# Quad 5's k and q: loaded earlier and transposed by DMA instead of TensorE

## The chip, the cores and the metric

The kernel runs on one core of a Trainium2 chip. The metric is the device time of one execution in microseconds. Of the kernel before there are three timed runs, and one more execution that the profiler recorded; the profile's own times count from the start of its span.

## The reference

Sigmoid attention over 8 batches, 12 heads, 448 positions and 64 dimensions per head, and behind it two matrix products with a SiLU between them. All inputs and the output are float32.

```python
def _attn_ref(q, k, v):
    S = q.shape[2]
    scale = 1.0 / np.sqrt(q.shape[-1])
    scores = scale * np.matmul(q, k.transpose(0, 1, 3, 2)) - np.log(S)
    attn = 1.0 / (1.0 + np.exp(-scores))
    return np.matmul(attn, v)

x = attn_out.transpose(0, 2, 1, 3).reshape(B * S, H * D)    # 3584 x 768
h = x @ w_in                                                # 768 x 2048
g = h * (1.0 / (1.0 + np.exp(-h)))
out = g @ w_out                                             # 2048 x 768
```

## The kernel before

**Quads.** Four heads of one batch are a *quad*; a batch has three (`NQ`), the whole problem 24. A quad's k, q and v are loaded (`load`, line 124, on GpSimd's DMA queue, with a cast to 16 bits) into tiles `kf`, `qf` and `vf`, three of each in rotation (`p3`): quad 5's tiles are those that quad 2 had, and quad 8's are those that quad 5 had.

**Transposes.** The scores need k and q with the head dimension on the partitions (`kT`, `qT`, three of each in rotation). There are two ways to get there. `pe_transpose` (line 196) multiplies the 14 blocks of a tile with the identity on TensorE into two PSUM banks, and two VectorE casts (line 203) move them to `kT` or `qT`. `dma_transpose` copies the tile once into another order of its elements (`kr`, `qr`, line 211, two of each in rotation), and a DMA on SP's queue (line 212) transposes that copy into `kT` or `qT`. Quads 0 to 5 take the first way, quads 6 to 23 the second.

**Units.** A quad has seven *units*, one per 64 keys. `scores` (line 225) makes one: four matmuls into a double PSUM bank `psc`, of which there are two in rotation in the first stage, and one ScalarE sigmoid (line 232) into `attnT`. `values` (line 256) multiplies the seven units of a quad with v, 28 matmuls into two single PSUM banks `pav`, and VectorE scales the sums into `xT` (line 267). Four single banks are in rotation in this stage, for `ptrk`, `ptrq`, `pav` and `ph`.

**h.** `h_unit` (line 288) makes one block of 128 of the 2048 columns of h for one batch: six matmuls of a part of w_in with `xT` into a bank `ph`. The last two of the six need the batch's third quad. For batch 0 ScalarE makes a sigmoid of the bank (`tx`, line 302) and VectorE multiplies the two (`gTr`, line 303), which frees the bank; for batch 1 ScalarE does it alone (SiLU, line 307). w_in is loaded in four quarters (`load_w_in`, line 155, four transfers each); the second quarter, `load_w_in(1)`, serves blocks 4 to 7.

**Order.** Every engine runs its instructions in the order in which the program emits them. In the first stage that order is a table: units 0 to 23 one by one (`for n in range(NT_B + 3)`), each followed by what `behind` lists for its number; there lie the transposes of quads 1 to 4, the values of quads 0 to 2 in pieces, and the first matmuls of h blocks 0 and 1 (`begin`). From unit 24 to unit 41 come *bursts* of two units (`burst`), each followed by the values of a finished quad, if there is one, and by eight or nine h matmuls (`stretch`). Quad 5's first unit is unit 35, the second of burst n=34. The transposes of quad 5 stood behind bursts n=26 (k) and n=30 (q). Loads are called from `after_transpose(g)` and `after_values(g)`, so their place on GpSimd's queue follows the places of those steps in the program; a load also waits until the tile it overwrites has been read.

After unit 41 and the values of quad 5, the rest of batch 0's and batch 1's h blocks follow; in between stand VectorE's sums of parts of w_in and w_out (`w_in_sums`, line 326, and `w_sums`, line 477) and the row copies of quads 6 to 8. Then come three stages in which the output products (`out_set`, line 504) of one pair of batches alternate with the scores and values of the next, each followed by the next pair's h (`h_pair`, line 378), and at the end the output products of the last pair.

Of the kernel before, what the change touches and what calls it, by code (L numbers as in the profile page):

```python
# [17 lines left out]
def kernel(  # L18
# [9 lines left out]
    nc = tc.nc  # L28
# [82 lines left out]
    def new_flat(name, g):  # L111
        flat[name, g] = p3.tile([P, 2, NCH, D], F16, tag=f"{name}f", name=f"{name}f")

    def rows_in(name, g):
        b, iq = divmod(g, NQ)
        return source[name][b, 4 * iq : 4 * iq + 4].rearrange(
            "(i h) (p c) d -> (h p) i (c d)", h=2, c=NCH
        )

    def load(names, g, c0=0, c1=NCH):  # L120
        for name in names:
            if (name, g) not in flat:
                new_flat(name, g)
            nc.gpsimd.dma_start(  # L124
                flat[name, g][:, :, c0:c1].rearrange("p i c d -> p i (c d)"),
                rows_in(name, g)[:, :, c0 * D : c1 * D],
            )
# [22 lines left out]
    def load_w_in(step):  # L150
        cols = slice(step * DFF // 4, (step + 1) * DFF // 4)
        rows = moe_w_in[:, cols].rearrange("(iq j h d) f -> h j d iq f", j=2, h=2, d=D)
        for half in range(2):
            for j in range(2):
                nc.gpsimd.dma_start(
                    w_in_sb[j * D : (j + 1) * D, half * NQ : (half + 1) * NQ, cols], rows[half, j]
                )
# [13 lines left out]
    def new_qkT(g):  # L171
        for name in ("k", "q"):
            qkT[name, g] = p3.tile([P, NCH, P], F16, tag=f"{name}T", name=f"{name}T")
# [14 lines left out]
    def pe_transpose(g, pieces=(("k", 0, 4), ("k", 4, NCH), ("q", 0, 4), ("q", 4, NCH))):  # L188
        if ("k", g) not in qkT:
            new_qkT(g)  # L190
        for name, c0, c1, *copy in pieces:
            dst = qkT[name, g].rearrange("p c t -> p (c t)")
            ptr = one_bank(f"ptr{name}")
            for c in range(c0, c1):
                for j in range(2):
                    nc.tensor.matmul(
                        ptr[j * D : (j + 1) * D, (c - c0) * P : (c - c0 + 1) * P],
                        flat[name, g][:, j, c, :],
                        ident,
                        start=True,  # L200
                        stop=True,
                    )
            (copy[0] if copy else nc.vector.tensor_copy)(  # L203
                dst[:, c0 * P : c1 * P], ptr[:, : (c1 - c0) * P]
            )

    def dma_transpose(g, name, copy):
        if ("k", g) not in qkT:
            new_qkT(g)
        rows = p2.tile([P, NCH, 2, D], F16, tag=f"{name}r", name=f"{name}r")  # L210
        copy(rows, flat[name, g].rearrange("p j c d -> p c j d"))
        nc.sync.dma_start_transpose(
            out=qkT[name, g], in_=rows.rearrange("p c j d -> p (c j d)")
        )
# [25 lines left out]
    def values(g, end=NCH):  # L240
        b, iq = divmod(g, NQ)
        if b not in xT:
            assert b < 2 or b - 2 in h_done
            xT[b] = p2.tile([P, NPAIR, S], F16, tag="xT", name="xT")
        pav, done_rounds = part_of.pop(g, None) or (None, 0)
        if pav is None and bufs_of["double"] > 2 and "any" not in banks:
            both = two_banks("pav")
            pav = [both[:, half] for half in range(2)]
        elif pav is None:
            pav = [one_bank("pav") for _ in range(2)]  # L250
        for ch in range(done_rounds, end):
            at = attnT.pop((g, ch))
            for half in range(2):
                own = slice(half * HP, (half + 1) * HP)
                for j in range(2):
                    nc.tensor.matmul(  # L256
                        pav[half][j * D : (j + 1) * D, :S],
                        flat["v", g][own, j, ch, :],
                        at[own, j, :],
                        start=(ch == 0),  # L260
                        stop=(ch == NCH - 1),
                    )
        if end < NCH:
            part_of[g] = pav, end
            return
        for half in range(2):
            nc.vector.tensor_scalar_mul(xT[b][:, half * NQ + iq, :], pav[half][:, :S], SX)  # L267
        if iq == NQ - 1:
            ready.add(b)
# [365 lines left out]
    def after_transpose(g):  # L635
        if g == 0:
            load("kq", 3)
        elif g == 1:
            load("kq", 4)
            load_w_in(0)  # L640
            load_w_in(1)
        elif g == 2:
            load("kq", 5)
        elif g == 5:
            load("kq", 8)

    def after_values(g):
        if g == 0:
            load("v", 3)
            load_w_in(2)  # L650
            load_w_in(3)
        elif g == 1:
            load("v", 4)
            load_w_out(0, 0)
            load_w_out(0, 1)
        elif g == 2:
            load("v", 5)
            load_w_out(1, 0)
            load_w_out(1, 1)
            load("kq", 6)  # L660
            load("kq", 7)
        elif g + 3 < NQB:
            load("v", g + 3)
        if g >= 2 * NQ and g % (2 * NQ) == 2 * NQ - 2:
            sums_of_x.append(x_sums(g // (2 * NQ), 0, NQ - 1))
# [14 lines left out]
    def rest_of_first_k():  # L680
        pe_transpose(0, (("k", FIRST, 4), ("k", 4, NCH)))
        after_transpose(0)

    def transposes(g, name):
        pe_transpose(g, ((name, 0, 4), (name, 4, NCH)))
        if name == "q":
            after_transpose(g)

    def rounds(g, end):
        values(g, end)  # L690
        if end == NCH:
            after_values(g)

    def begin(fc, steps):
# [11 lines left out]
        8: ((transposes, 2, "k"),),  # L706
        9: ((transposes, 2, "q"),),
        10: ((rounds, 0, 3),),
        11: ((rounds, 0, 7),),
        12: ((transposes, 3, "k"),),  # L710
        13: ((transposes, 3, "q"),),
        14: ((rounds, 1, 2),),
        15: ((rounds, 1, 4),),
        16: ((rounds, 1, 7),),
# [1 line left out]
        18: ((transposes, 4, "q"),),  # L716
        19: ((rounds, 2, 3),),
        20: ((rounds, 2, 6),),
        21: ((begin, 0, 4),),
        22: ((rounds, 2, 7),),  # L720
        23: ((begin, 1, 4),),
    }
    for n in range(NT_B + 3):
# [6 lines left out]
    def stretch(stream, ns, spent=0):  # L730
        nonlocal done, due
        due += ns
        done += spent
        while done < due:
            step_ns = next(stream, None)
            if step_ns is None:
                return
            done += step_ns

    def burst(n, size=2):  # L740

        new = units[n : n + size]
        for u in new:
            scores(*u)
        with_values = values_if_any()
        for g, ch in new:
            if ch == NCH - 1:
                waiting.append(g)
                if 9 <= g + 3 < NQB:
                    later.extend(((g + 3, "k"), (g + 3, "q")))  # L750
        return with_values
# [2 lines left out]
    stretch(stream, 1600)  # L754
    for n in range(NT_B + 3, 2 * NT_B, 2):
        burst(n)
        if n in (26, 30):
            transposes(5, "k" if n == 26 else "q")
        stretch(stream, 1600)
    values_if_any()  # L760
    for _ in stream:
# [5 lines left out]
    for m in range(B // 2 - 1):  # L767
# [11 lines left out]
        left, n = 0.0, 2 * NT_B * (m + 1)  # L779
# [62 lines left out]
```

## Time and profile before

| what | value |
|---|---|
| three timed runs | 368.84, 369.35, 369.56 us, median 369.35 |
| profiled execution: its own time | 369.54 us |
| its span in the profile | 367.6 us |
| granted TensorE clock | full over the whole span |
| data moved by DMA | 42.78 MB, mean 116 GB/s |
| scores' sigmoid (line 232) | 168 instructions, 1009 ns each |
| h matmul (line 288) | 192 instructions, 353 ns each, overlapping |
| k and q DMA transposes (line 212) | 18 each, median 3.5 us (k) and 4.6 us (q) to landing |

The first stage, with everything up to the last h block of batch 1, ends near 76 us. Busy times per engine over parts of it, in us, with what the DMA engines moved:

| stretch, us | TensorE | VectorE | ScalarE | DMA, GB/s |
|---|---|---|---|---|
| 20 to 25 | 4.93 | 3.97 | 5.00 | 203 |
| 25 to 30 | 5.00 | 1.69 | 4.89 | 204 |
| 30 to 35 | 4.63 | 2.73 | 4.35 | 202 |
| 35 to 40 | 5.00 | 2.79 | 3.79 | 203 |
| 40 to 45 | 5.00 | 2.31 | 4.65 | 207 |
| 45 to 50 | 4.56 | 2.85 | 4.54 | 202 |
| 50 to 55 | 5.00 | 2.75 | 4.03 | 204 |

A timeline line gives the start, the length from the first start to the last end, the engine, the source line and the operation with what it writes and reads. Lengths of neighbours on one engine overlap, so what a piece of work takes from its engine is read from start to start. What an engine waited for stands in brackets behind the line. "To landing" is the time from the issue of a transfer to its end.

### The profile page before, as it was taken

To read this page: it belongs to the slowest core of one execution; us is meant where nothing else is said; L and a number is where in the kernel's file an instruction comes from. 1 tells how busy PE (TensorE), PEld (TensorE's weight loads), DVE (VectorE), ACT (ScalarE), POOL (GpSimd) and SP (SyncE) were. 2 spreads that over 40 slices of the span, in tenths; PEclk is the share of its full clock that TensorE was granted. 3 is DMA by queue.
4 is the path that set the end of the run, shared out by engine and by line. 5 is a ranking of instruction groups with operands and counts; after the bars stand their busy time and mean duration, and the time that the engine had idled before them with its cause. 6 is when DMAs were issued, how large, how long until landed. Compare 5 with 4: busy or idle time off the path is not lost. (4 is left out here: it accounts for less than half of the span.)

```text
span 367.6 us, 7594 instructions
## 1 busy us (share of the span) xinstructions
PE 359.3 (98%) x3009; PEld 183.8 (50%) x3009; DVE 251.8 (69%) x458; ACT 250.0 (68%) x339; POOL 77.5 (21%) x116
## 2 busy tenths in 40 slices
PE   7999999999999999999999999999999999999995
PEld 3554445545544555545445555554455555555552
DVE  2565559957756587867665768795756677797763
ACT  5998886479998756687777846679998956640000
POOL 8566521040061172000041047000100000000000
PEclk9999999999999999999999999999999999999999
DMA  8999999987989599007589359922863020003333
GB/s 132 198 204 202 204 203 204 197 115 134 153 114 223 117 135 177 2 0 162 92 168 206 61 128 129 135 24 51 151 113 86 19 71 0 3 0 86 87 86 85
DMA packets 65858, 42.78 MB, mean 116 GB/s; under 512 B 36128, under 2 KB 62496, under 8 KB 65824
## 3 DMA queue, kind: packets, MB, share of 16 engines
q0 software_dynamic: 27072, 22.58, 43.0%
q1 hardware_dynamic: 38320, 19.34, 27.0%
q8 instruction: 23, 0.38, 0.4%
q10 hardware_dynamic: 432, 0.39, 0.3%
q14 instruction: 11, 0.09, 0.1%
HBM read 45.61 MB, written 11.01 MB: 154 GB/s over the span
## 5 line engine op out<-in xcount | busy, mean ns | idle before, releaser
L232 ACT ACTIVATE attnT<-psc,bias_s 128x896 f16<-128x896 f32 x168 | 158.1, 1009 | 21.9 <-PE psc L225 21.6
L504 PEld LDWEIGHTS <-S 128*128 128x128 f16 x448 | 41.3, 98 | 36.5 <-issue 8.1
L225 PE MATMUL psc<-qT,kT 64*64 64x448 f16 x672 | 51.1, 362 | 1.4 <-DVE kT L203 0.5
L267 DVE TENSOR_SCALAR xT<-pav 128x448 f16<-128x448 f32 x48 | 27.7, 619 | 32.5 <-PE pav L256 32.5
L124 POOL DMA_DIRECT2D vf<-in_v_dram x24 | 17.3, 721 | 136.0 <-PE pav L256 118.1
L504 PEld LDWEIGHTS <-gTr 128*128 128x128 f16 x336 | 31.3, 98 | 26.6 <-issue 7.7
L504 PE MATMUL po<-T,S 128*128 128x384 f16 x224 | 42.0, 327 | 0.2
L504 PE MATMUL po<-w_out_sb,gTr 128*128 128x384 f16 x224 | 41.6, 327 | 0.0
L378 PEld LDWEIGHTS <-w_in_sb 128*128 128x128 f16 x288 | 27.9, 98 | 26.7 <-issue 1.1
L504 PE MATMUL po<-w_out_sb,S 128*128 128x384 f16 x224 | 40.8, 326 | 0.0
L256 PE MATMUL pav<-attnT,vf 64*64 64x448 f16 x672 | 38.3, 350 | 0.5 <-DVE gTr L303 0.4
L288 PE MATMUL ph<-xT,w_in_sb 128*128 128x448 f16 x192 | 38.7, 353 | 0.1
L378 PE MATMUL pa<-xT,w_in_sb 128*128 128x448 f16 x144 | 33.1, 353 | 0.0
L225 PEld LDWEIGHTS <-kT 64*64 64x64 f16 x672 | 17.8, 104 | 28.7 <-issue 22.3
L378 PEld LDWEIGHTS <-SI 128*128 128x128 f16 x216 | 21.1, 98 | 20.0 <-issue 0.5
L256 PEld LDWEIGHTS <-vf 64*64 64x64 f16 x672 | 21.0, 107 | 13.3 <-issue 3.8
L288 PEld LDWEIGHTS <-w_in_sb 128*128 128x128 f16 x192 | 17.8, 98 | 19.1 <-issue 3.7
L394 ACT ACTIVATE part<-pa 128x448 f32<-128x448 f32 x24 | 13.1, 544 | 19.2 <-PE pa L378 18.3
L504 PE MATMUL po<-T,gTr 128*128 128x384 f16 x112 | 22.1, 327 | 0.0
L372 ACT ACTIVATE gTr<-pc 128x448 f16<-128x448 f32 x24 | 13.1, 544 | 12.9 <-DVE pc L388 12.5
L388 DVE TENSOR_TENSOR part<-pb,part 128x448 f32<-128x448 f32 x24 | 14.9, 621 | 8.3 <-ACT part L394 5.0
L186 ACT ACTIVATE m<-po 128x384 f32<-128x384 f32 x1 | 0.5, 491 | 27.7 <-PE po L504 27.7
(75 smaller groups left out, 468.2 us busy)
## 6 DMA issues: line engine op xcount, KB each, us to landing
out_dram<-osb SPq DMA_DIRECT2D x52, 192.0 KB, 3.0
vf<-in_v_dram POOLq DMA_DIRECT2D x24, 224.0 KB, 6.5
kf<-in_k_dram POOLq DMA_DIRECT2D x23, 224.0 KB, 6.9
qf<-in_q_dram POOLq DMA_DIRECT2D x23, 224.0 KB, 7.4
w_in_sb<-in_moe_w_in_dram POOLq DMA_DIRECT2D x16, 192.0 KB, 8.1
w_out_sb<-in_moe_w_out_dram POOLq DMA_DIRECT2D x4, 768.0 KB, 14.9
out_dram<-osb SPq DMA_DIRECT2D x6, 96.0 KB, 2.1
kT<-kr SPq DMA_TRANSPOSE x18, 3.5
```

The lines of the kernel that those rows point to most:

```text
L124: nc.gpsimd.dma_start(flat[name, g][:, :, c0:c1].rearrange("p i c d -> p i (c d)"), rows_in(name, g)[:, :, c0 * D : c1 * D],)
L186: nc.scalar.activation(o, i, AF.Copy)
L225: nc.tensor.matmul(psc[own, j, :S], qkT["k", g][rows, ch, own], qkT["q", g][rows, :, own], start=True, stop=True,)
L232: nc.scalar.activation(attnT[g, ch], psc[:, :, :S], AF.Sigmoid, bias=bias_s, scale=QKSCALE)
L256: nc.tensor.matmul(pav[half][j * D : (j + 1) * D, :S], flat["v", g][own, j, ch, :], at[own, j, :], start=(ch == 0), stop=(ch == NCH - 1),)
L267: nc.vector.tensor_scalar_mul(xT[b][:, half * NQ + iq, :], pav[half][:, :S], SX)
L288: nc.tensor.matmul(ph[:, :S], w_in_sb[:, cc, fc * P : (fc + 1) * P], xT[b][:, cc, :], start=(at == 0), stop=(at == NCC - 1),)
L372: nc.scalar.activation(gTr[:, r * NG + i, col + c * S : col + (c + 1) * S], h, AF.Silu, bias=0.0, scale=ISX)
L378: nc.tensor.matmul(to, w[:, n, i * P : (i + 1) * P], x[:, n], start=(start and n == 0), skip_group_check=not start, stop=(n == NQ - 1),)
L388: nc.vector.tensor_add(o, po, x)
L394: nc.scalar.activation(got[i, 1], bank[i, "a"], AF.Copy)
L504: nc.tensor.matmul(po[:, :NO2], a[:, fc, :], w[:, fc, :], start=(fc == 0), stop=(fc == NHC - 1))
```

## The change

The second quarter of w_in is issued behind quad 5's k and q instead of ahead of them. Quad 5 no longer passes through TensorE: VectorE copies its k rows ahead of the scaling of quad 2 and its q rows behind it (`rows_of_5`, in the places of units 21 and 22), and SP's queue transposes both. Behind the q rows stands `after_transpose(5)`, which loads quad 8's k and q; that call moves with it from burst n=30 to unit 22, so on GpSimd's queue these two loads now stand ahead of the load of quad 6's v.

```diff
@@ after_transpose
         elif g == 1:
             load("kq", 4)
             load_w_in(0)
-            load_w_in(1)
         elif g == 2:
             load("kq", 5)
+            load_w_in(1)
         elif g == 5:
             load("kq", 8)
@@
+    def rows_of_5(name):
+        dma_transpose(5, name, nc.vector.tensor_copy)
+        if name == "q":
+            after_transpose(5)
@@ behind
         18: ((transposes, 4, "q"),),
         19: ((rounds, 2, 3),),
         20: ((rounds, 2, 6),),
-        21: ((begin, 0, 4),),
-        22: ((rounds, 2, 7),),
+        21: ((rows_of_5, "k"), (begin, 0, 4)),
+        22: ((rounds, 2, 7), (rows_of_5, "q")),
         23: ((begin, 1, 4),),
@@
     for n in range(NT_B + 3, 2 * NT_B, 2):
         burst(n)
-        if n in (26, 30):
-            transposes(5, "k" if n == 26 else "q")
         stretch(stream, 1600)
```

## The prediction

> **What bounds the kernel now.** I read the busy shares first, then TensorE's waits, then each engine's timeline over the stretch that the edit touches (20 to 60 us), then the transfers.
>
> ```profile
> span 367.6 us, 7594 instructions
> ...
> PE 359.3 (98%) x3009; PEld 183.8 (50%) x3009; DVE 251.8 (69%) x458; ACT 250.0 (68%) x339; POOL 77.5 (21%) x116
> ```
>
> TensorE has work for 98% of the span, so what is taken out of its order shows up at the end, unless another engine then holds it. Its list of waits has six entries for the whole span, and two of them lie in the stretch:
>
> ```profile
> PE pav L256 <- DVE gTr L303: 0.4, 1, 0.4
> PE ptrk L196 <- DVE gTr L303: 0.4, 1, 0.4
> ```
>
> The second waits inside the transposes that go away. TensorE's timeline (start, length, work):
>
> ```profile
> 32.51 0.71 PE L225 MATMUL psc<-qT,kT 64*64 64x448 f16 x8
> 33.16 0.41 PE L196 MATMUL ptrk<-ident,kf 128*64 128x128 f16 x8
> 33.94 0.36 PE L196 MATMUL ptrk<-ident,kf 128*64 128x128 f16 x6 [0.37 <-DVE gTr L303]
> 34.23 1.88 PE L288 MATMUL ph<-xT,w_in_sb 128*128 128x448 f16 x9
> ...
> 39.98 0.58 PE L196 MATMUL ptrq<-ident,qf 128*64 128x128 f16 x14
> 40.50 1.88 PE L288 MATMUL ph<-xT,w_in_sb 128*128 128x448 f16 x9
> ...
> 44.43 0.66 PE L225 MATMUL psc<-qT,kT 64*64 64x448 f16 x8
> ...
> 48.02 1.51 PE L256 MATMUL pav<-attnT,vf 64*64 64x448 f16 x26 [0.44 <-DVE gTr L303]
> ```
>
> The k transposes hold TensorE from 33.16 to 34.23 (1.07 us, wait included), the q transposes from 39.98 to 40.50 (0.52 us). The burst at 44.43 (n=34) is the first with a unit of quad 5. ScalarE in the same stretch:
>
> ```profile
> 35.38 0.55 ACT L302 ACTIVATE tx<-ph 128x448 f16<-128x448 f32 x1
> 36.47 1.91 ACT L232 ACTIVATE attnT<-psc,bias_s 128x896 f16<-128x896 f32 x2 [0.54 <-PE psc L225]
> ...
> 42.74 1.91 ACT L232 ACTIVATE attnT<-psc,bias_s 128x896 f16<-128x896 f32 x2 [0.35 <-PE psc L225]
> ...
> 46.74 1.01 ACT L302 ACTIVATE tx<-ph 128x448 f16<-128x448 f32 x2
> ```
>
> It is nearly as full as TensorE: its waits on the bursts are only 0.54 and 0.35 us. The wait of 0.44 us at TensorE's 48.02 is ScalarE's doing: that bank holds h block 9, which VectorE (L303) can release only after the sigmoid at 46.74.
>
> **The change, part by part.** *Removed:* 28 matmuls and 28 weight loads, four PSUM banks taken, and four VectorE casts (two pairs of 1.15 us). TensorE's order shortens by 1.07 + 0.52 = 1.59 us, the upper bound of the gain.
>
> How much ScalarE lets through I work out burst by burst. Two score banks take turns, so a burst's second unit waits for the second sigmoid of the burst before; a sigmoid is 0.95 us and the short one 0.45 us from start to start.
> - n=28, now at 36.03, comes up at 34.96. Its second unit waits for the sigmoid that ends at 35.46. The short sigmoid then runs to 35.9, so the pair of n=28 starts at 35.83 instead of 36.47. TensorE goes on to the values about 35.7 instead of 36.44: 0.74 of the 1.07 us is left.
> - n=30 comes at 38.7; behind it the h matmuls follow at 39.24 instead of 40.50. n=32 comes at 41.1, but ScalarE still has the pair of n=30 (39.3 to 41.2) and a short one to do: the pair of n=32 starts at 41.7 instead of 42.74, without its 0.35 us of idle time.
> - n=34 would come at 43.2; its second unit waits for 43.6. The pair of n=34 runs 44.05 to 45.95 instead of 44.96 to 46.88, the short sigmoid of block 9 starts at 45.95, VectorE releases the bank at 47.1, and TensorE goes on at 47.1 instead of 48.02.
>
> So from 48 us on **0.9 us** remain: ScalarE's two idle times, 0.54 + 0.35. Behind that each pair has at least 0.5 us of room (bursts 2.3 to 4.3 us apart), and from 57 us TensorE waits for nobody. The four missing banks shift the ring of four by two between n=26 and n=30 and then bring it round again, so block 9 meets the same bank. I take 0.9, ends 0.5 and 1.6.
>
> *Added on VectorE:* two copies, by their own row 0.61 us, in the holes around quad 2's scaling:
>
> ```profile
> 24.23 1.14 DVE L203 CAST qT<-ptrq 128x512 f16<-128x512 f32 x2
> 27.58 1.16 DVE L267 TENSOR_SCALAR xT<-pav 128x448 f16<-128x448 f32 x2 [2.20 <-PE pav L256]
> 29.84 1.15 DVE L303 SCALAR_TENSOR_TENSOR gTr<-ph,tx 128x448 f16<-128x448 f32 x2 [1.10 <-ACT tx L302]
> ...
> 62.44 0.61 DVE L211 COPY kr<-kf 128x896 f16<-128x896 f16 x1
> ```
>
> The k copy has 25.37 to 27.58, the q copy 28.74 to 29.84: hidden if quad 5's k lands by 26.9 and q by 29.2. Behind a late k copy the scaling waits, and h block 0's last two matmuls (at about 28.5) wait for that, one us for one.
>
> *Moved on POOL's queue:* quad 5's two loads go ahead of w_in(1)'s four. The queue keeps eight transfers in flight; each issue waits for the one eight before it.
>
> ```profile
> 17.50 0.63 POOL L155 DMA_DIRECT2D w_in_sb<-in_moe_w_in_dram  x1 [0.61 <-DMA kf<-in_k_dram]
> ...
> 22.22 0.74 POOL L124 DMA_DIRECT2D kf<-in_k_dram  x1 [0.24 <-PE pav L256]
> ```
>
> In the 17.50 and 18.57 places k and q land about where w_in(1)'s first two did (25.4, 26.4) plus 32 KB each: 25.6 and 26.8. Their buffers were quad 2's, transposed by 16.4. w_in(1)'s four then land at 27.7 to 30.7 instead of 25.4 to 28.5: 448 KB at the 203 GB/s of this stretch is 2.25 us. Block 4's first matmul, the last before burst n=26, wants the first half at 32.3; its second, behind that burst, wants the rest at 33.2.
>
> *Added on SP:* two transposes, at about 26.4 and 29.4, on a queue otherwise empty until 62 us. In 62 to 72 us, where they run beside loads, all traffic together keeps the loads' rate:
>
> ```profile
> DMA packets 5672, 2.05 MB, mean 205 GB/s; under 512 B 4659, under 2 KB 5672, under 8 KB 5672
> ```
>
> So each displaces 224 KB, 1.1 us: w_in(1) ends by 31.8, v of quad 3 lands at 32.1 + 2.3 = 34.4 (wanted at 35.7), w_in(2) at 38.3 (wanted at 40.4), v of quad 5 at 52.1 (wanted at 54.6). The first two transposes of that later stretch landed in 5.6 and 4.9 us, all of them in 2.9 to 13.7: k at 32, q at 35, wanted at 43.6.
> The Trainium skill, page "VectorE: DVE Perf Modes", section "The three transpose paths", puts a 128x128 transpose at 390 ns on TensorE and 1309 ns by DMA, and advises TensorE where PSUM will do. By its figure seven blocks are an estimated 9.2 us, both tiles 18.3 us, so q would land at 44.7 and burst n=34 wait 1.1 us, an end of 369.5 us; the landings of 5.6 and 4.9 us do not agree.
>
> *Moved too:* quad 8's two loads go ahead of v of quad 6 on POOL's queue. v of quad 6 is issued near 57.5 instead of 49.18 and, at the 8.6 us of its neighbours, lands at 66; its values start at 85.9. Quad 6's loads land near 61.5 by the displaced 2.3 us (59.1 now); VectorE may wait 0.7 us for them, but it has 3.84 us of idle time at 73.6.
>
> **Sum.** The profiled execution took 369.54 us, 1.94 more than its span: 369.54 - 0.9 = 368.64. The median of the runs, 369.35, lies 0.19 below it, so I predict 369.35 - 0.9 = **368.45 us**.
>
> **Rivals.** *All of it:* ScalarE does not hold TensorE, since h blocks or score banks pace differently from my starts: 369.35 - 1.59 = 367.75. For it: TensorE's 98%. Against: ScalarE's gaps add up to less.
> *Half is given back:* ScalarE, full from 35 to 47 us, catches up only with the values, so q's 0.52 is wholly lost and part of k's too: 369.35 - 0.5 = 368.85. For it: bursts n=30 to 36 come 2.1 to 2.8 us apart against ScalarE's 2.4 to 2.8 us of work.
> *Quad 5's q lands late:* the longest q landing, 12.0 us, gives 41.4, still ahead of 43.6; it decides from 14.2 us on. At 15.3 us it gives back 1.1: 369.55.
> *Slower, by loads pushed back:* if a transpose costs the loads three times its bytes while both run (3.4 us instead of 1.1), w_in(1) ends at 34.1 and TensorE waits 0.9 us at block 4; v of quad 3 lands at 39.0 against 36.6, 2.4 us more: 369.35 - 0.9 + 3.3 = 371.75. It decides from about 1.8 us each (v of quad 3 at 35.7); at 2.7 us TensorE waits 0.2 and 1.6 us, +0.9 in all, 370.25. Against: 205 GB/s beside transposes. For it: all margins here are 1.3 us.
> *Slower, because the load is no earlier:* if k lands at its old 29.4, the scaling starts at 30.0 instead of 27.58: 369.35 - 0.9 + 2.4 = 370.85. Against: landings in the stretch are 7.1 to 8.7 us, and 9.4 would be needed.
>
> **How the numbers follow.** Forecast 0.45, all of it 0.12, half 0.18, q late 0.05, loads pushed back 0.14, load no earlier 0.06. About 0.2% (0.74 us) is what a measurement can tell from no change, so faster is below 368.6. The forecast lies just below that line and run-to-run differences put a fifth of it above: faster 0.36 + 0.12 + 0.04 of "half" = 0.52; same 0.09 + 0.14 + 0.05 = 0.28; slower 0.20. The range runs from 367.6 (all of it, and 0.15 of scatter) to 370.4 (loads pushed back at 2.7 us, and the same scatter), which leaves out the worst of the two slow cases and little below. The forecast's own range is 368.0 to 368.9.
>
> **What would show it.** In the profile after: no L196 work past 24 us; k copies of quad 5 near 25.7 and the scaling still at 27.6; the pair of sigmoids of n=28 near 35.8; TensorE's wait before the values of quad 4 still there, ending near 47.1; first product (L504) near 75.1 instead of 75.97; span near 366.7. I am wrong if TensorE waits on w_in_sb or vf at 32 to 36 us, on kT or qT near 43.6, or if the scaling starts after 28 us.

## The result and the profile after

| | before | after |
|---|---|---|
| median of 22 runs each | 369.48 us | 370.07 us |
| ratio of the times, 95% interval | | 1.0020 (1.0011 to 1.0028) |
| profiled execution: own time, span | 369.54, 367.6 us | 371.07, 369.0 us |
| first h matmul behind the values of quad 5 | 57.01 us | 55.88 us |
| first output product | 75.97 us | 75.64 us |
| output product ahead of quad 6's values | 84.59 us | 86.11 us |

The change made the kernel slower by 0.2%. One of the 22 executions after, 411.1 us at a granted clock of 0.85, is left out of the ratio. The profiled execution lies 1.0 us above the median of its kernel, so the late waits in it are larger than in a typical one; it shows where they are. TensorE's work, from its timeline, before and then after:

```profile
57.01 19.13 PE L288 MATMUL ph<-xT,w_in_sb 128*128 128x448 f16 x99
75.97 2.44 PE L504 MATMUL po<-w_out_sb,gTr 128*128 128x384 f16 x14
...
79.18 1.30 PE L504 MATMUL po<-T,S 128*128 128x384 f16 x7
...
84.59 0.98 PE L504 MATMUL po<-w_out_sb,S 128*128 128x384 f16 x5
```

```profile
55.88 19.13 PE L288 MATMUL ph<-xT,w_in_sb 128*128 128x448 f16 x99
75.64 2.44 PE L504 MATMUL po<-w_out_sb,gTr 128*128 128x384 f16 x14 [0.63 <-ACT gTr L307]
...
79.25 1.31 PE L504 MATMUL po<-T,S 128*128 128x384 f16 x7 [0.25 <-DVE S L515]
...
86.11 0.97 PE L504 MATMUL po<-w_out_sb,S 128*128 128x384 f16 x5 [1.27 <-DVE osb L528]
```

TensorE was 1.13 us ahead of the kernel before at 56 us. Ahead of the first output product 0.80 of it went, at the third product (79.25, before 79.18) nothing of it was left, and the wait at 86.11 put it 1.52 us behind. That distance it kept, about: 1.4 us at the end of the span. So the stage that was changed got faster, and the three waits behind it gave more than that back. VectorE's timeline after shows what was late:

```profile
25.81 0.62 DVE L211 COPY kr<-kf 128x896 f16<-128x896 f16 x1 [0.37 <-DMA kf<-in_k_dram]
27.64 1.16 DVE L267 TENSOR_SCALAR xT<-pav 128x448 f16<-128x448 f32 x2 [1.21 <-PE pav L256]
...
61.40 0.56 DVE L477 TENSOR_TENSOR T<-w_out_sb 128x768 f16<-128x768 f16 x1 [1.42 <-DMA w_out_sb<-in_moe_w_out_dram]
...
63.30 0.62 DVE L211 COPY kr<-kf 128x896 f16<-128x896 f16 x1 [0.40 <-DMA kf<-in_k_dram]
...
73.33 0.62 DVE L211 COPY kr<-kf 128x896 f16<-128x896 f16 x1 [4.08 <-DMA kT<-kr]
...
84.98 0.62 DVE L211 COPY kr<-kf 128x896 f16<-128x896 f16 x1 [1.77 <-DMA kf<-in_k_dram]
```

Quad 5's k copy fits its hole, and the scaling starts at 27.64, on time. The third copy below (73.33) is quad 8's: it overwrites the rows of quad 6, two of each being in rotation, and so waits 4.08 us for quad 6's transpose. All of `w_sums` that stands behind it is late. Before, that wait was 0.47 us:

```profile
68.84 0.62 DVE L211 COPY kr<-kf 128x896 f16<-128x896 f16 x1 [0.47 <-DMA kT<-kr]
```

The gate on GpSimd's queue is a copy of one element of quad 8's `qT`; the loads of quads 9 to 11 stand behind it. SP's queue after, and the gate after and then before:

```profile
26.52 1.32 SPq L212 DMA_TRANSPOSE kT<-kr  x1
29.35 3.93 SPq L212 DMA_TRANSPOSE qT<-qr  x1
64.01 1.22 SPq L212 DMA_TRANSPOSE kT<-kr  x1
65.32 3.63 SPq L212 DMA_TRANSPOSE qT<-qr  x1
69.04 3.78 SPq L212 DMA_TRANSPOSE kT<-kr  x1
```
```profile
78.63 1.55 POOL L568 COPY gate<-qT 1x1 f16<-1x1 f16 x1 [14.10 <-DMA qT<-qr]
```
```profile
74.03 0.18 POOL L568 COPY gate<-qT 1x1 f16<-1x1 f16 x1 [13.67 <-DMA qT<-qr]
```

Quad 6's two transposes landed 9.2 and 8.7 us after issue; before it was 5.6 and 4.9. The k transpose, before and then after:

```profile
kT<-kr SPq DMA_TRANSPOSE x1, 5.6
```
```profile
kT<-kr SPq DMA_TRANSPOSE x1, 9.2
```

The gate, which waits for quad 8's, opened at 78.63 instead of 74.03, and quad 9's k was issued at 80.12 instead of 74.51. VectorE waited 1.77 us for that load at 84.98, with the sum of line 528 queued behind the copy, and TensorE waited 1.27 us for the bank that this sum reads. The added transposes themselves (times to landing, k and q of quad 5):

```profile
kT<-kr SPq DMA_TRANSPOSE x1, 11.5
...
qT<-qr SPq DMA_TRANSPOSE x1, 14.5
```

### The profile page after: what moved, and what is told of

Its sections match the earlier page's. It is cut to its first block, busy times and chain, and to the rows that moved or that the text cites. A ratio compares the mean times of both kernels' runs of the same rounds, so it can differ in the third digit from the quotient of the medians.

```text
span 369.0 us, 7541 instructions
## 1 busy us (share of the span) xinstructions
PE 359.0 (97%) x2981; PEld 183.1 (50%) x2981; DVE 250.9 (68%) x456; ACT 250.0 (68%) x339; POOL 78.8 (21%) x116
## 5 line engine op out<-in xcount | busy, mean ns | idle before, releaser
L124 POOL DMA_DIRECT2D kf<-in_k_dram x25 | 18.0, 722 | 8.9 <-DMA w_out_sb<-in_moe_w_out_dram 3.4
```

The lines of the kernel that those rows point to most:

```text
L124: nc.gpsimd.dma_start(flat[name, g][:, :, c0:c1].rearrange("p i c d -> p i (c d)"), rows_in(name, g)[:, :, c0 * D : c1 * D],)
```

## The experiments

Each was timed against the kernel before on the same chip (369.38 to 369.49 us there, so that a difference between runs of two chips carries up to 0.11 us from that).

| run | median, us | ratio to before, 95% interval |
|---|---|---|
| no transposes of quad 5 | 368.91 | 0.9991 (0.9982 to 1.0000) |
| no transposes, spare bank | 368.21 | 0.9969 (0.9958 to 0.9980) |
| changed, spare bank | 369.69 | 1.0008 (0.9996 to 1.0020) |
| changed, own rows for quad 8 | 369.44 | 1.0009 (0.9992 to 1.0026) |
| changed, v of quads 6 to 8 deferred | 369.11 | 0.9988 (0.9979 to 0.9997) |
| changed, v deferred, spare bank | 368.42 | 0.9968 (0.9957 to 0.9978) |
| before, two more transposes | 370.21 | 1.0020 (1.0011 to 1.0029) |
| before, load order alone | 369.45 | 1.0001 (0.9993 to 1.0010) |
| before, v deferred | 369.55 | 1.0003 (0.9994 to 1.0012) |
| changed, v deferred, spare bank, q copy early | 368.36 | 0.9973 (0.9961 to 0.9985) |
| changed, v deferred, spare bank, old load order | 372.27 | 1.0076 (1.0063 to 1.0089) |

**TensorE's gain without the transfers.**

```diff
-            transposes(5, "k" if n == 26 else "q")
+            name = "k" if n == 26 else "q"
+            qkT[name, 5] = qkT[name, 4]
+            if name == "q":
+                after_transpose(5)
```


> The kernel before without the transposes of quad 5, on either path: quad 5's scores use quad 4's k and q (this part of the computation is left out), all loads stand where they stood. Theory: TensorE gains 1.1 us by 56 us, as in the profile after, and gives 0.8 us back ahead of the first output product, because the same four banks are missing and the last h block lands in the bank that the first product takes; no transfers are added, so nothing else is lost: 369.48 - 0.3 = 369.2. Rival (all that is lost comes from the transfers): 369.48 - 1.1 = 368.4.

Measured 368.91 us. By the medians that is 0.6 us below before, by the ratio 0.3 us, as expected, with an interval that reaches 1.0000. The wait ahead of the first product is there, as in the changed kernel:

```profile
75.41 2.44 PE L504 MATMUL po<-w_out_sb,gTr 128*128 128x384 f16 x14 [0.63 <-ACT gTr L307]
```

**The bank.** The four single banks are not handed out in a strict turn. In the programs as built the last h block of batch 1 has bank 5 in the kernel before and bank 6 without the transposes, in the changed kernel too; the first output product takes bank 6 in all of them. So without the transposes that product has to wait for the last SiLU, and in the kernel before only for an earlier one. A spare matmul turns the order (the last h block then has bank 5 again):

```diff
+    def spare_bank():
+        nc.tensor.matmul(
+            one_bank("pw")[:, :64], dummy[:, :P], dummy[:, :64], start=True, stop=True
+        )
...
         burst(n)
+        if n == 38:
+            spare_bank()
         stretch(stream, 1600)
```


> The same, with one spare bank taken (a matmul of 64 columns) behind burst n=38, so that the last h block lands in another bank than the first output product's. Theory: no wait ahead of the first product, 369.48 - 1.1 = 368.4, and 0.8 us less than the run without the spare bank. Rival (the bank does not matter): the same time as the run without it.

Measured 368.21 us: 0.70 below the run without the spare bank, with intervals that do not overlap, and the wait is gone (TensorE's timeline, the same product group):

```profile
74.38 2.44 PE L509 MATMUL po<-w_out_sb,gTr 128*128 128x384 f16 x14
```

So 1.28 us (369.49 - 368.21; 1.15 by the ratio) is what taking quad 5 off TensorE is worth, and 0.70 us is what the bank takes back.

> The changed kernel with that same spare bank. Theory: the wait of 0.63 us ahead of the first product goes, 370.07 - 0.8 = 369.3 if VectorE's late sums do not take its place. Rival (VectorE's sums, 4.5 us late in the profile after, hold the products all the same): 370.0, with the time lost at the third product instead.

Measured 369.69 us; its interval overlaps that of the changed kernel, so the timing alone doesn't tell the two apart. The profile does: the first product no longer waits, but VectorE holds the third and TensorE then waits again.

```profile
78.81 1.31 PE L509 MATMUL po<-T,S 128*128 128x384 f16 x7 [0.95 <-DVE S L520]
...
84.72 0.97 PE L509 MATMUL po<-w_out_sb,S 128*128 128x384 f16 x5 [0.32 <-DVE osb L533]
```

Against the run without transposes and with the same spare bank, it is 1.48 us slower (369.69 - 368.21): that is the price of the transfers.

**Where the transfers cost.** First, rows of their own for quad 8:

```diff
+        if g == 8:
+            room = cpool.tile([P, NHC, P], F16, tag="S3" if name == "k" else "S4", name="own")
+            room = room.rearrange("p f t -> p (f t)")[:, : NCH * 2 * D]
+            rows = room.rearrange("p (c j d) -> p c j d", c=NCH, j=2)
+        else:
+            rows = p2.tile([P, NCH, 2, D], F16, tag=f"{name}r", name=f"{name}r")
```


> The changed kernel with rows of their own for quad 8's copies, so that VectorE does not wait there for quad 6's transposes. Theory: the 4.08 us wait goes, the sums and the gate of the next loads come 2 to 4 us earlier, the waits of 0.25 and 1.27 us at the products go, the bank's 0.63 us stays: 369.48 - 0.3 = 369.2. Rival (the transposes are slow on SP's queue itself, so the gate stays at 78 us): the wait of 1.27 us stays and the time is 369.8 or more.

In the profile the 4.08 us wait is gone and so are TensorE's waits for VectorE but one of 0.2 us; the gate still opens at 77.97, as the rival had it for that part. The ratio's interval (0.9992 to 1.0026) spans no change, and overlaps the changed kernel's: the time is not shown to improve. Waiting for the row buffer was one link, and SP's queue is late without it too.

Then the loads beside the transposes:

```diff
-        elif g + 3 < NQB:
+        elif 6 <= g < NQB - 3:
             load("v", g + 3)
@@ behind the gate
                         for to in (9, 10, 11):
                             load("kq", to)
+                            load("v", to - 3)
```


> The changed kernel with the loads of v of quads 6 to 8 behind the gate, one after each of the k and q loads of quads 9 to 11, so that they do not run beside the transposes of quads 6 to 8. Theory: those transposes land in 3 to 6 us again instead of 9, the gate opens near 74 us, the late chain is gone, the bank's wait stays: as the run without transposes, 368.9. Rival (the transposes are slow behind each other, whatever loads run): 370.

Measured 369.11 us, faster than before, with an interval wholly below that of the changed kernel. Quads 6 to 8 landed in a median of 3.6 (k) and 3.1 us (q), and quad 8's copy and the gate are back:

```profile
69.49 0.62 DVE L211 COPY kr<-kf 128x896 f16<-128x896 f16 x1 [0.25 <-DMA kT<-kr]
```
```profile
74.83 0.18 POOL L568 COPY gate<-qT 1x1 f16<-1x1 f16 x1 [19.76 <-DMA qT<-qr]
```

> The same with the spare bank. Theory: the whole gain of TensorE shows, 368.2, as in the run without transposes and with the spare bank. Rival: 369.7, as the changed kernel with the spare bank alone.

Measured 368.42 us: the best version that leaves nothing out (the earlier q copy below is level with it), 0.3% faster than before and 1.65 us below the changed kernel. Quad 5's q still comes late in it: its transpose lands at 44.55, and TensorE waits for it ahead of quad 5's first unit.

```profile
44.68 0.38 PE L230 MATMUL psc<-qT,kT 64*64 64x448 f16 x4 [1.04 <-DMA qT<-qr]
```

Does the deferral gain by itself?

> The kernel before, with nothing but the loads of v of quads 6 to 8 behind the gate. Theory: TensorE waits for none of what these loads delay in the kernel before, so the time stays 369.45 within 0.2, and the gain of the run with the change, this and the spare bank belongs to the change. Rival (the deferred loads are a gain of their own): 368.9 or less.

No: 369.55 us. It only removes what the change had added.

**The transfers alone.** Two row copies of quad 4 and two transposes into an unused tile, added to the kernel before:

```diff
-        21: ((begin, 0, 4),),
-        22: ((rounds, 2, 7),),
+        21: ((extra, 0, "k"), (begin, 0, 4)),
+        22: ((rounds, 2, 7), (extra, 1, "q")),
```


> The kernel before, with two more row copies (of quad 4) and two more DMA transposes in the places where the change puts them, into a tile that nobody reads; TensorE still transposes quad 5. Theory: the transposes of quads 6 to 8 are as late as in the changed kernel (gate near 78 us), but TensorE arrives 1.1 us later too, so most of the lateness is hidden: 369.5 to 370.2, about 369.8. Rival (the transfers cost the same 1.5 us wherever TensorE stands): 371.0.

Measured 370.21 us, at the upper end of what the theory allowed, above its central 369.8. The late chain is the changed kernel's: quad 8's copy waits 4.21 us and the gate opens at 79.26. In the profiled execution (369.91 us) TensorE's only new wait for it is 0.17 us; the slower executions left no trace, so how their time divides stays open. The DMA engines' rate from 26 to 44 us (the last column, GB/s), before and then here:

```profile
26.00:44.00 18.00, 17.63 (x170) 8.05 (x167) 9.15 (x16) 15.68 (x22) 11.34 (x16) 1.00 1.26 203
```
```profile
26.00:44.00 18.00, 17.63 (x169) 8.07 (x167) 9.68 (x17) 15.68 (x22) 9.91 (x14) 1.00 1.26 188
```

The changed kernel's own rate there is 188 GB/s too. Over 18 us, 15 GB/s are 0.27 MB that were not moved, on top of the transposes' own 0.46 MB. In the changed kernel two thirds of that fall into one microsecond, 3 us after the second transpose was issued; before and then after:

```profile
32.00:33.00 1.00, 1.00 (x12) 0.34 (x9) 0.00 (x0) 1.00 (x2) 0.60 (x1) 1.00 1.25 198
```
```profile
32.00:33.00 1.00, 1.00 (x12) 0.34 (x10) 0.00 (x0) 1.00 (x2) 0.00 (x0) 1.00 0.58 21
```

In the six other runs that issue both transposes before 30 us this microsecond has 42 to 131 GB/s.

**The order of the loads.**

> The kernel before with quad 5's k and q loaded ahead of the second quarter of w_in and nothing else. Theory: no wait on w_in appears near 32 us and the time is that of before, 369.5 within 0.2. Rival (the second quarter lands too late): a wait on w_in_sb and 370.5 or more.

Measured 369.45 us, no wait on w_in. And the old order with all the rest of the best version:

```diff
         elif g == 1:
             load("kq", 4)
             load_w_in(0)
+            load_w_in(1)
         elif g == 2:
             load("kq", 5)
-            load_w_in(1)
```


> The changed kernel with the deferred loads of v and the spare bank, but with quad 5's k and q loaded behind the second quarter of w_in again. Theory: VectorE's k copy waits for its load until 29.4, the scaling of quad 2 starts at 30.1 instead of 27.64, and h block 0 waits one us for one: 368.42 + 2.4 = 370.8. Rival (VectorE and TensorE make it good by the values of quad 3): 369 or less.

Measured 372.27 us, 3.85 above the best version, more than the 2.4 expected. VectorE's copy and TensorE behind it:

```profile
29.72 0.62 DVE L216 COPY kr<-kf 128x896 f16<-128x896 f16 x1 [4.28 <-DMA kf<-in_k_dram]
30.26 1.14 DVE L272 TENSOR_SCALAR xT<-pav 128x448 f16<-128x448 f32 x2
```
```profile
30.92 3.48 PE L293 MATMUL ph<-xT,w_in_sb 128*128 128x448 f16 x9 [2.22 <-DVE xT L272]
```

The scaling starts 2.6 us late, and TensorE stands idle 2.22 us for it. Behind that wait nine h matmuls take 3.48 us instead of 1.88, and the profile shows why: the TensorE clock granted over 31 to 34 us is 0.50 (the column `PEclk`, third from the end), where the best version has 1.00 over the same matmuls.

```profile
31.00:34.00 3.00, 3.00 (x8) 1.02 (x8) 2.18 (x4) 1.09 (x2) 1.35 (x3) 0.50 1.23 202
```

The next burst starts at 34.33 instead of 30.45, 3.88 us later: 2.2 us are the wait and 1.6 us the nine matmuls at the lower clock (3.41 us from 30.92 to 34.33, against 1.81 in the changed kernel from 33.22 to 35.03). All five executions of this version had a mean clock of 0.993 to 0.995, those of the best version 0.997 to 1.000. That the idle time brought the clock down is the order in which the trace shows them, not tested by itself; the wait of 1.27 us in the changed kernel left the clock at 1.00. Loading quad 5 earlier is free by itself, and in these places necessary for the row copies.

**An earlier q copy.**

```diff
-        22: ((rounds, 2, 7), (rows_of_5, "q")),
+        22: ((rows_of_5, "q"), (rounds, 2, 7), (after_transpose, 5)),
```


> The changed kernel with the deferred loads of v and the spare bank, and the q row copy of quad 5 ahead of the scaling of quad 2 instead of behind it. Theory: the q transpose is issued up to 1.3 us earlier, the wait of 0.7 to 1.0 us for it at burst n=34 goes, and the scaling starts 0.2 us later: 368.42 - 0.5 = 367.9. Rival (the transpose lands when the loads beside it are through, whenever it is issued): 368.4 to 368.7.

Measured 368.36 us, the same as without it: the time is the rival's. Its mechanism held by half. Issued 1.63 us earlier (27.72 instead of 29.35), the q transpose took 16.0 us to land, at 43.7, against 44.55 (29.35 + 15.2) in the best version, so 0.85 us of the 1.63 arrived. TensorE's wait fell from 1.04 to 0.38 us and the profiled execution is 0.38 us shorter (368.13 against 368.51), but the medians do not show a gain.

## Why the prediction was wrong

The forecast was 368.45 us, 0.9 us faster; measured were 370.07 us, 0.6 us slower.

- **TensorE's gain, 0.9 us:** right in kind, a little small. The profile after has 1.13 us at 56 us, and the run without transposes and bank wait is 1.28 us faster. ScalarE did hold TensorE as worked out: the pair of n=28 started at 35.80 (predicted 35.83).
- **The row copies, and quad 5's loads ahead of w_in(1):** right. k was copied at 25.81 (predicted near 25.7), the scaling started at 27.64, w_in was not waited for, and the order alone costs nothing. The price named for a late k copy, one for one, was too low: 2.6 us of lateness cost 3.85 us, 1.6 of them in matmuls at a granted clock of 0.50.
- **"The four missing banks ... bring it round again":** this step failed. The banks do not go round in a strict turn, so four takes fewer do not restore the order. The last h block got the first product's bank: 0.70 us.
- **"So each displaces 224 KB, 1.1 us", and the landings of 5.6 and 4.9 us:** this step failed as well. The rows of the profile behind it came from 62 to 72 us, where the loads were running out. Beside a queue of loads kept full, the two transposes landed in 11.5 and 14.5 us, and quad 6's k arrived at 63.3 (43.30 + 20.0) instead of 59.1 (39.10 + 20.0), 4.2 us later where 2.3 was in the sum. q of quad 5 landed at 43.85, against "wanted at 43.6", and quad 5's first unit waited 0.37 us ahead of 44.01, the sign of being wrong that the prediction names. (The view puts this wait to ScalarE; the best version has it longer, 1.04 us, and puts it to the q transpose.) It cost nothing in the end: by 56 us TensorE was 1.13 us ahead. By its figure for a 128x128 transpose by DMA, the Trainium skill (page "VectorE: DVE Perf Modes", section "The three transpose paths") gave an estimate of 44.7, nearer than mine. But quad 8's transposes, of the same size, landed in 3.0 and 2.9 us when issued at 74.34 and 75.67 in the same execution, where that figure gives an estimated 9.2 us each; so what sets the time here is what runs beside them, not a fixed price per block.
- **"VectorE may wait 0.7 us for them, but it has 3.84 us of idle time":** the step with the largest consequence. It counted quad 6's loads and stopped there. Behind them stand quad 6's transposes, the row buffer that quad 8's copy takes from them (4.08 us), the gate (4.6 us late) and quad 9's load (1.77 us at VectorE, 1.27 us at TensorE). In the timed runs the transfers cost 1.48 us.
- **The sum:** 1.28 us gained, 1.48 lost to the transfers, and 0.38 to the bank on top of them (370.07 - 369.69, a difference within the intervals): 0.6 us slower, as measured between before and after. Alone the bank takes 0.70 us; beside VectorE's late sums a part of its wait is hidden.
- **The rivals:** none had the bank. "Slower, by loads pushed back" had the kind of the other loss right, transposes that cost the loads more than their bytes (4.2 us for two, where the sum had 2.3), and its place wrong: it adds up waits at block 4 and at v of quad 3, which the profile after does not have. What came late were transfers from 61 us on, and TensorE waited behind them at 79 and 86 us. That its 370.25 lies near the measured 370.07 is luck.

## What to carry to other kernels

Transfers added to a stretch whose DMA queue is full may not be paid there but, as here, where the backlog ends: follow it to the first transfers behind it that somebody waits for, and through every buffer and gate that these release. An instruction taken away can also move every later buffer of its pool; see which buffer the next stage's first instruction gets. Once the loss is located, moving loads that nobody needs yet out of the backlog can cost nothing and bring the gain back: 368.42 us here, 0.9968 (0.9957 to 0.9978) of the time before.

## What the hardware showed that I had not expected

Two DMA transposes of 224 KB beside loads that keep eight transfers in flight landed 10.8 to 16.0 us after their issue in the profiles of these runs, and in the changed kernel the DMA engines moved 188 instead of 203 GB/s over the 18 us around them, with the rate down to 21 GB/s in one of these microseconds. Issuing the second one earlier by 1.63 us made it land earlier by 0.85 us. With the loads gone, a transpose of the same size took 2.9 to 3.0 us. Why the total rate falls was not tried.

A wait of TensorE can cost more than its length: behind one of 2.22 us the granted clock was 0.50 for 3 us, and nine matmuls took 1.6 us more than at the full clock.
